# Eighteen subtractions moved from GpSimd to VectorE, and eight scalar products from GpSimd to ScalarE, in an attention and mixture-of-experts kernel

## The chip, the cores and the metric

One of the eight cores of one Trainium2 chip runs the whole program. The metric is device time in microseconds (us). Before the change the kernel takes 1013.66 us, the median of three runs (1013.41 to 1014.27). Engines are named as in the profile: PE is TensorE's matmul, PEld its weight load, DVE is VectorE, ACT is ScalarE, POOL is GpSimd, SP is the engine that issues most DMAs.

## The reference

Two parts follow each other. The first is attention inside clusters, for 4 batches of 8 heads, 768 tokens and 64 numbers a head:

```
q_assign = argmax(normalized q . normalized centroids);  k_assign likewise
scores = q . k^T / sqrt(64), -1e9 where the two clusters differ
attn   = softmax(scores);   attn_out = attn . v
```

The second takes the 3072 tokens with all their heads side by side (512 numbers) as x:

```
logits = x @ w_gate + log1p(exp(x @ w_noise)) * noise
the two best of 8 experts per token, softmax weights over these two
out[token] += weight * (relu(x @ w1[e]) @ w2[e])
```

## The kernel before, in words

Numbers of 32 bits are carried as two halves of 16 bits (upper and lower), and each product is three matmuls of halves, so nearly every tile has a step that makes its upper half and one that subtracts to get the lower.

The attention works through 16 pairs of heads, numbered 0 to 15 (`p`); four pairs are a batch `b`. A pair has 12 steps: two heads (`s`) by six blocks of 128 keys (`kc`); step number `i = 6*s + kc`. I write 7/2 for step 2 of pair 7. A step does this:

- `scores` (L641, L642): PE multiplies one key block with all 768 queries (four matmuls of 384 columns), ACT takes the exponential into a 32-bit tile `pe` of 128 by 768.
- `split_p` (L653): the upper 16 bits of `pe` are used in place as the upper half; one TENSOR_TENSOR subtracts them from `pe` and writes the lower half `pl`. It has two inputs in SBUF. It stands on POOL, except for the last nine steps of pair 14 and all of pair 15, where it stands on DVE. It is issued one step after its `scores` (two or three steps late in a few steps near the end).
- `values` (L670, L672, L676), four to five steps later: PE multiplies both halves with the halves of v and adds up in the tile `av`; 18 small matmuls, the last six with `pl`. After a head's last block DVE normalizes: `rs` (L682, from `av` and the factor `ch`), its reciprocal (L683), and the product into `xt` (L685). There is one `av` tile, so the next head's first L670 waits for L685.

Beside these steps run the preparations for the next pair: transposes of q and k (L511) with their halves on ACT (L524) and DVE (L525), the search for the cluster (L543 to L566 on the PSUM tile `aux`, ending in `oh`, which L575 transposes into the mask), and the row maxima (`b_max`: L611 on PE, L613 on DVE, two of each a step). Once per batch come the sizes of v, its halves (L467, L468 on ACT, L469 on POOL), and `x_scale`, whose last part `heads` writes the two numbers `ch` of a partition: `am` times `xsc` (L455). Pair 0 uses `am` itself; from pair 1 on L682 needs `ch`. The two writes stand once per batch, in pairs 1, 4, 8 and 12.

The second half's routing is spread under the attention: each pair's output is split (L720, L721) and stored, transposed back (L1189) and multiplied with the gate (L739); `g_gate` is a chain of small DVE steps on `aux`; and when a batch's places are known, twelve list writes (`g_list`, L898 and L899: a MEMSET of one number and an indirect DMA, both on POOL) put its tokens into the table `tbl`. For batch 0 these fall into pairs 7 to 9, for batch 1 into pairs 11 to 13, for batch 2 into pairs 14 and 15. After some 460 us the experts start; from there on PE is busy without a pause.

The order on each engine is written by hand: `at(step, f)` puts each piece into a third of a step by the numbers of the table `AT`, and every engine executes its own instructions in that order. The main loop is

```
slot(0)
scores(t)
split_p(t - 1)
slot(1)
values of step t - 4
slot(2)
```

The PSUM buffers `ring` (six of them) go round among `scores`, `b_max`, the transposes and the small products, so a reader that is late holds up a PE matmul some six buffers later.

Of the kernel before, what the change touches and what calls it, by code (L numbers as in the profile page):

```python
# [14 lines left out]
AF = mybir.ActivationFunctionType  # L15
OP = mybir.AluOpType
# [19 lines left out]
    vd=[1, 1, 2, 3, 4, 5], sec=-6.0, qf=[0, -4.0], place1=4.333,  # L36
    fv=[{'v': -5.0, 'vscale': 13.0, 'am': 24.333, 'amstep': 0.333, 'vsplit': 25.333, 'vstep': 2.0},
        {'v': 9.0, 'vscale': 11.667, 'am': 13.333, 'amstep': 0.333, 'xs': 14.0, 'vsplit': 15.0, 'vstep': 1.0}],
    wmax=42, thr=0.333, bmax1=14.667, bstep1=0.5)


def rap(tensor, offset, dims):
# [3 lines left out]
class Kernel:  # L46
# [402 lines left out]
    def x_scale(self, b):  # L449
        nc = self.nc  # L450

        def heads():
            self.ch[b] = self.wk.tile([128, 2], F32, name="ch")
            for g in range(2):
                nc.gpsimd.tensor_scalar(self.ch[b][:, g:g + 1], self.am[b, g][:, 1:2], self.xsc[:, b, 0:1], None,  # L455
                                        op0=OP.mult)

        return self.power_root(self.wk, lambda: self.vm[b], lambda: self.xsc[:, b], 2) + [heads]

# [185 lines left out]
    def split_p(self, p, s, kc):  # L645

        nc, st = self.nc, self.st[p]
        pe = st["p", s, kc].rearrange("p a n -> p (a n)")
        hi = pe.bitcast(BF).rearrange("p (n two) -> p n two", two=2)[:, :, 1]
        lo = self.wk.tile([128, self.S], F16, name="pl", bufs=5)  # L650

        last = p == self.NP - 1 or (p == self.NP - 2 and 6 * s + kc >= 3)
        (nc.vector if last else nc.gpsimd).tensor_tensor(lo, pe, hi, op=OP.subtract)  # L653
        st["p", s, kc] = hi, lo

    def values(self, p, s, kc):
# [674 lines left out]
```

## Time and profile before

| what | us |
|---|---|
| median of three runs | 1013.66 |
| the profiled execution's own time | 1013.59 |
| its span, first to last instruction | 1011.8 |
| PE busy in the span | 928.7 (92%) |
| DVE busy | 660.6 (65%) |
| POOL busy | 565.7 (56%) |
| ACT busy | 473.4 (47%) |

The span of the profile is 1.79 us shorter than that execution's own time, and this execution is within 0.1 us of the median. The shares are means over two parts with different limits: up to some 460 us all four engines are loaded, behind it PE alone. The busy time of PE is modelled at the matmuls' ends, so a PE that is busy throughout may still follow another engine's pace. A number in brackets at the end of a timeline row is the idle time of the engine before it, with what ended it.

### The profile page before, as it was taken

Reading aid. Unit: us, or ns where it says so; the run is one execution under the profiler, and the core shown is the slowest. Engines: PE = TensorE matmul, PEld = TensorE weight load, DVE = VectorE, ACT = ScalarE, POOL = GpSimd, SP = SyncE. Lnnn points to the kernel's source line nnn. Section 1 sums busy time; section 2 is a strip of 40 time slices with the busy share of each in tenths; the row PEclk is TensorE's granted clock in tenths of the full one; section 3 lists DMA queues with packets and bytes.
Section 4 is the critical chain, followed back from the end, with each engine's and each line's share of the span. In section 5 each row is a group of like instructions: output and inputs, shape, how many; then the busy total and the mean of one; then the engine's idle time right before and its main releaser. Section 6 shows DMA issues by size and latency. Waiting matters only on the chain.

```text
span 1011.8 us, 22606 instructions
## 1 busy us (share of the span) xinstructions
PE 928.7 (92%) x8825; PEld 560.4 (55%) x8825; DVE 660.6 (65%) x1485; ACT 473.4 (47%) x896; POOL 565.7 (56%) x608
## 2 busy tenths in 40 slices
PE   4588989898899987889999999999999999999997
PEld 3356666666666664668555445455454454554543
DVE  6688777888678876897556465365564654655631
ACT  4578788888787865674032224123131241231310
POOL 9268797979997899853456125242261252422312
PEclk7699999999999998999999999999999999999999
DMA  6543767666667444668377645655665356555201
GB/s 178 125 118 89 194 156 185 183 165 145 179 153 189 119 95 98 204 152 176 109 150 242 137 142 167 140 174 149 173 193 140 126 165 152 172 151 155 73 24 46
DMA packets 181905, 148.84 MB, mean 147 GB/s; under 512 B 93543, under 2 KB 159079, under 8 KB 181794
## 3 DMA queue, kind: packets, MB, share of 16 engines
q1 hardware_dynamic: 167990, 110.73, 43.8%
q0 software_dynamic: 13296, 36.38, 11.7%
q8 instruction: 70, 1.15, 0.5%
q10 hardware_dynamic: 508, 0.25, 0.1%
q14 instruction: 41, 0.34, 0.1%
HBM read 81.80 MB, written 26.12 MB: 107 GB/s over the span
## 4 chain that ended last, share of the span: by engine, by line
PE 57%; POOL 10%; DVE 9%; issue 9%; ACT 6%; DMA 4%; SPq 0%; ACTq 0%; POOLq 0%; DVEq 0%
PE ring L1230 21%; PE ring L1270 20%; POOL pl L653 6%; PE ring L641 5%; ACT pe L642 3%; DVE mm L613 3%; PE ring L611 2%; POOL tbl L899 2%; DMA B<-nt 2%; PE av L670 1%; PE av L676 1%; PE av L672 1%; POOL out L1283 1%; PE ring L1260 1%; DVE pl L653 1%
## 5 line engine op out<-in xcount | busy, mean ns | idle before, releaser
L653 POOL TENSOR_TENSOR pl<-pe 128x768 f16<-128x768 f32 x171 | 247.9, 1468 | 47.4 <-ACT pe L642 41.9
L1230 PE MATMUL ring<-xT,w1t 128*128 128x404 f16 (+2 forms) x1632 | 267.1, 324 | 0.0
L1270 PE MATMUL ring<-w2t,hT 128*128 128x512 f16 x1152 | 250.8, 379 | 0.5 <-DVE w2t L1166 0.5
L642 ACT ACTIVATE pe<-ring,sc 128x384 f32<-128x384 f32 x384 | 200.0, 577 | 69.1 <-PE ring L641 62.0
L613 DVE TENSOR_REDUCE mm<-ring 128x1 f32<-128x384 f32 x384 | 192.1, 549 | 44.6 <-PE ring L611 44.0
L1283 POOL DMA_INDIRECT out<-yo,idx x52 | 58.7, 1129 | 285.4 <-DVE yo L1279 209.3
L1230 PEld LDWEIGHTS <-w1t 128*128 128x128 f16 x1632 | 157.4, 97 | 106.4 <-issue 2.5
L1270 PEld LDWEIGHTS <-hT 128*128 128x128 f16 x1152 | 112.4, 98 | 135.0 <-issue 1.2
L1239 ACT ACTIVATE hT<-ring 128x404 f16<-128x404 f32 (+2 forms) x136 | 57.6, 469 | 202.1 <-PE ring L1230 201.9
L641 PE MATMUL ring<-B 128*128 128x384 f16 x384 | 127.2, 332 | 3.6 <-DMA B<-nt 3.6
L641 PE MATMUL ring<-A 128*128 128x384 f16 x384 | 126.8, 330 | 3.6 <-ACT pe L642 2.1
L611 PE MATMUL ring<-A 128*128 128x384 f16 x384 | 105.2, 334 | 16.5 <-ACT pe L642 8.0
L1240 DVE SCALAR_TENSOR_TENSOR hT<-ring,hT 128x404 f16<-128x404 f32 (+2 forms) x136 | 66.7, 529 | 73.5 <-ACT hT L1239 73.5
L1279 DVE SCALAR_TENSOR_TENSOR yo<-ring,lsw,xt 128x512 f32<-128x512 f32 (+1 forms) x49 | 36.7, 748 | 110.2 <-PE ring L1270 104.3
L670 PE MATMUL av<-vv,pe 128*128 128x65 f16 x1152 | 96.9, 194 | 7.5 <-DVE xt L685 7.4
L672 PE MATMUL av<-vv,pe 128*128 128x64 f16 x1152 | 96.9, 193 | 0.0
L670 PEld LDWEIGHTS <-pe 128*128 128x128 bf16 x1152 | 83.7, 98 | 22.9 <-issue 9.3
L1165 ACT ACTIVATE w1t<-stg,ws 128x1024 f16<-128x1024 f32 x32 | 34.5, 1139 | 121.2 <-DVE ws L170 121.2
L672 PEld LDWEIGHTS <-pe 128*128 128x128 bf16 x1152 | 78.4, 99 | 11.3 <-issue 4.7
L676 PE MATMUL av<-vv,pl 128*128 128x65 f16 x1152 | 66.8, 194 | 5.6 <-POOL pl L653 4.2
L1210 POOL DMA_INDIRECT xh<-xs,idx x52 | 56.4, 1085 | 16.5 <-issue 15.0
L1154 DVE TENSOR_REDUCE wm<-stg 128x1 f32<-128x1024 f32 x56 | 65.5, 1208 | 0.0
(227 smaller groups left out, 1171.0 us busy)
## 6 DMA issues: line engine op xcount, KB each, us to landing
stg<-in_moe_w SPq DMA_DIRECT2D x64, 512.0 KB
vt<-in_v SPq DMA_DIRECT2D x8, 768.0 KB
out<-zt SPq DMA_DIRECT2D x12, 512.0 KB
A<-hl SPq DMA_DIRECT2D x30, 192.0 KB
B<-hl SPq DMA_DIRECT2D x30, 192.0 KB
xs<-xh SPq DMA_DIRECT2D x15, 384.0 KB
qk<-in_q SPq DMA_DIRECT2D x7, 768.0 KB
qk<-in_k SPq DMA_DIRECT2D x7, 768.0 KB
```

Of the source, the lines that this page charges most:

```text
L611: nc.tensor.matmul(t, A[:, 0, s, j * 128:j * 128 + 128], A[:, 1, s, n * 384:n * 384 + 384], start=True, stop=True)
L613: nc.vector.tensor_reduce(st["mm"][:, c, n:n + 1], t, axis=X, op=OP.max, negate=True)
L641: nc.tensor.matmul(t, M[:, 1 - qi, s, ks], M[:, qi, s, ns], start=not qi, stop=bool(qi))
L642: nc.scalar.activation(pe[:, n], t, AF.Exp, bias=math.log(64.0), scale=st["sc"][:, 4:5])
L653: (nc.vector if last else nc.gpsimd).tensor_tensor(lo, pe, hi, op=OP.subtract)
L670: nc.tensor.matmul(av[:, j, :], ph[:, js], vv[:, hh, kj, 64:129], start=(kc == 0 and j == 0), stop=False, skip_group_check=True)
L672: nc.tensor.matmul(av[:, j, :64], ph[:, js], vv[:, hh, kj, 0:64], start=False, stop=False, skip_group_check=True)
L676: nc.tensor.matmul(av[:, j, :], pl[:, js], vv[:, hh, kj, 64:129], start=False, stop=(kc == NJ - 1), skip_group_check=True)
L1230: nc.tensor.matmul(p, self.w1t[:, wi, c, f * 128:f * 128 + 128], self.xT[:, c, xi, n0:n1], start=(i == 0), stop=(i == 3 * ND - 1))
L1240: nc.vector.scalar_tensor_tensor(h1, x, 0.0, h0, op0=OP.max, op1=OP.subtract)
L1270: nc.tensor.matmul(p, self.hT[:, hi, f, t * 128:t * 128 + 128], self.w2t[:, wi, f], start=(i == 0), stop=(i == 3 * NF - 1))
L1283: i = nc.gpsimd.indirect_dma_start(out=self.out, out_offset=bass.IndirectOffsetOnAxis(ap=en[:r], axis=0), in_=yo[:r], in_offset=None, boun ...
```

## The change

In six pairs (7, 8, 9, 11, 12, 13) the steps 2, 6 and 10 take their lower half on DVE instead of POOL: 18 of the 171 that stand on POOL. And `heads` writes `ch` by two ACTIVATEs on ACT instead of two TENSOR_SCALARs on POOL, once per batch.

```
-    wmax=42, thr=0.333, bmax1=14.667, bstep1=0.5)
+    wmax=42, thr=0.333, lists=(7, 8, 9, 11, 12, 13), bmax1=14.667, bstep1=0.5)
...
             for g in range(2):
-                nc.gpsimd.tensor_scalar(self.ch[b][:, g:g + 1], self.am[b, g][:, 1:2], self.xsc[:, b, 0:1], None,
-                                        op0=OP.mult)
+                nc.scalar.activation(self.ch[b][:, g:g + 1], self.am[b, g][:, 1:2], AF.Copy, scale=self.xsc[:, b, 0:1])
...
-        last = p == self.NP - 1 or (p == self.NP - 2 and 6 * s + kc >= 3)
-        (nc.vector if last else nc.gpsimd).tensor_tensor(lo, pe, hi, op=OP.subtract)
+        i = 6 * s + kc
+        vector = (p == self.NP - 1 or (p == self.NP - 2 and i >= 3) or
+                  (p in AT["lists"] and i % 4 == 2))
+        (nc.vector if vector else nc.gpsimd).tensor_tensor(lo, pe, hi, op=OP.subtract)
```

The changed file has one line fewer between L455 and L650 and one more behind that: what was L613 is L612 there, L653 is L654, L682 is L683, L898 is L899. PE and SP keep their order.

On DVE, in pair 7 around step 3 (mm are the row maxima, mx the first step of the cluster search), before:

```order
L849 SCALAR_TENSOR_TENSOR rec<-aux,xsc,gm 128x6
L613 TENSOR_REDUCE mm<-ring 128x1 x6
L549 TENSOR_REDUCE mx<-aux 128x24
L495 TENSOR_REDUCE ring<-ring 128x2
L182 TENSOR_SCALAR ring<-ring 128x2
L497 TENSOR_SCALAR sc<-ring 128x2
```

The same place with the change:

```order
L850 SCALAR_TENSOR_TENSOR rec<-aux,xsc,gm 128x6
L612 TENSOR_REDUCE mm<-ring 128x1 x4
L654 TENSOR_TENSOR pl<-pe 128x768
L612 TENSOR_REDUCE mm<-ring 128x1 x2
L548 TENSOR_REDUCE mx<-aux 128x24
L494 TENSOR_REDUCE ring<-ring 128x2
```

The split of 7/2 now stands ahead of two row maxima and of the whole cluster search. Those of 7/6 and 7/10 stand likewise between row maxima, the first of them behind `oh`.

On POOL, in pair 7 where batch 0's list writes begin (vv is the lower half of v, tbl the table), before:

```order
L653 TENSOR_TENSOR pl<-pe 128x768 x2
L469 TENSOR_TENSOR vv<-vt,vv 128x12x64
L898 MEMSET spacer 1x1
L899 DMA tbl<-rec,pk 32768x2
L653 TENSOR_TENSOR pl<-pe 128x768 x2
```

With the change:

```order
L654 TENSOR_TENSOR pl<-pe 128x768 x2
L468 TENSOR_TENSOR vv<-vt,vv 128x12x64
L899 MEMSET spacer 1x1
L900 DMA tbl<-rec,pk 32768x2
L654 TENSOR_TENSOR pl<-pe 128x768
```

Between two list writes stand now one split and two splits in turn, where there were always two.

On ACT, in pairs 4, 8 and 12 (hl are the halves of q and k of the next pair), with the change:

```order
L641 ACTIVATE pe<-ring,sc 128x384 x2
L523 ACTIVATE hl<-ring,sc 128x384
L455 ACTIVATE ch<-am,xsc 128x1 x2
L523 ACTIVATE hl<-ring,sc 128x384
L641 ACTIVATE pe<-ring,sc 128x384 x2
```

Before, the two of hl followed each other and `ch` stood on POOL between two splits.

## Rows read from the trace of the kernel before

**Rows 1.** The chain that ended last, 236 to 281 us, its shares by line.
```profile
by line: POOL pl L653 58.1%; POOL tbl L899 18.4%; POOL xh L721 7.1%; issue 5.8%; ACT pe L642 3.6%; PE ring L641 1.5%; DVE xt L685 1.3%; PE av L670 1.2%; PE av L672 0.8%; PE av L676 0.8%; POOL ch L455 0.6%; DVE rs L682 0.5%; POOL spacer L898
```

**Rows 2.** Pairs 7, 8 and 12: stretch, length, busy PE, PEld, DVE, ACT, POOL, then clock.
```profile
225.90:252.10 26.20, 23.26 (x368) 16.76 (x365) 22.34 (x60) 22.11 (x42) 22.53 (x23) 1.00 0.62 148
252.10:280.70 28.60, 23.25 (x371) 17.04 (x368) 19.47 (x51) 22.08 (x42) 27.25 (x31) 1.00 0.76 180
...
358.70:387.80 29.10, 24.98 (x389) 17.80 (x386) 19.92 (x53) 16.81 (x35) 27.76 (x31) 0.94 0.52 104
```

**Rows 3.** Who waited for whom: us in total, times, the longest.
```profile
DVE rs L682 <- POOL ch L455: 7.6, 2, 3.8
...
PE av L676 <- POOL pl L653: 4.2, 6, 0.9
...
PE aux L543 <- DVE gm L798: 2.2, 1, 2.2
...
PE ring L739 <- DMA xhT<-xh: 1.6, 1, 1.6
```

**Rows 4.** The end of pair 8 in order of time: POOL, DVE, PE.
```profile
278.15 0.30 POOL L455 TENSOR_SCALAR ch<-am,xsc 128x1 f32<-128x1 f32 x1
...
278.49 0.23 DVE L682 TENSOR_SCALAR rs<-av,ch 128x6 f32<-128x6 f32 x1 [3.81 <-POOL ch L455]
...
279.58 0.19 PE L670 MATMUL av<-vv,pe 128*128 128x65 f16 x1 [3.05 <-DVE xt L685]
```

**Rows 5.** Stretches of 4 us; the last three numbers are PE's granted clock, DMA share, GB/s.
```profile
279.00:283.00 4.00, 3.42 (x53) 2.50 (x53) 3.05 (x7) 3.57 (x6) 3.81 (x5) 0.73 0.78 158
...
383.00:387.00 4.00, 3.49 (x37) 1.95 (x38) 1.84 (x6) 0.58 (x3) 3.82 (x7) 0.57 0.54 142
```

**Rows 6.** The tile pl: duration in ns, least, median, most.
```profile
L653 POOL TENSOR_TENSOR pl<-pe x171: 1457/1468/1486, 46.1 to 425.8; 128x768 f16<-128x768 f32 x171
L653 DVE TENSOR_TENSOR pl<-pe x21: 942/951/2335, 423.5 to 458.7; 128x768 f16<-128x768 f32 x21
```

**Rows 7.** Two DVE splits that met a POOL split, in order of time.
```profile
422.65 1.48 POOL L653 TENSOR_TENSOR pl<-pe 128x768 f16<-128x768 f32 x1
...
423.48 1.47 DVE L653 TENSOR_TENSOR pl<-pe 128x768 f16<-128x768 f32 x1
...
425.81 2.33 DVE L653 TENSOR_TENSOR pl<-pe 128x768 f16<-128x768 f32 x1
...
425.83 1.49 POOL L653 TENSOR_TENSOR pl<-pe 128x768 f16<-128x768 f32 x1
```

**Rows 8.** Pair 7, steps 2 to 4, in order of time: ACT, POOL, DVE, PE.
```profile
232.45 1.03 ACT L642 ACTIVATE pe<-ring,sc 128x384 f32<-128x384 f32 x2
...
233.42 1.59 POOL L469 TENSOR_TENSOR vv<-vt,vv 128x768 f16<-128x768 f32 x1
...
232.08 1.02 DVE L613 TENSOR_REDUCE mm<-ring 128x1 f32<-128x384 f32 x2 [0.91 <-PE ring L611]
234.06 1.02 DVE L613 TENSOR_REDUCE mm<-ring 128x1 f32<-128x384 f32 x2 [0.95 <-PE ring L611]
...
240.74 0.45 PE L575 MATMUL ring<-identb,oh 128*128 128x128 bf16 x5 [0.74 <-DVE oh L566]
```

**Rows 9.** Pair 7, step 7, and the start of pair 8: DVE and PE.
```profile
243.78 0.62 DVE L525 SCALAR_TENSOR_TENSOR hl<-ring,sc,hl 128x384 f16<-128x384 f32 x1
...
244.82 0.49 PE L511 MATMUL ring<-ident,qk 128*128 128x128 f32 x3
...
254.04 0.56 DVE L613 TENSOR_REDUCE mm<-ring 128x1 f32<-128x384 f32 x1 [2.42 <-PE ring L611]
```

**Rows 10.** The small ACTIVATE nearest in form to the new ch.
```profile
L845 ACT ACTIVATE rec<-aux,xsc 128x6 f32<-128x6 f32 x4 | 1.1, 272 | 4.8 <-DVE pk L844 4.8
```

**Rows 11.** POOL held by a DVE operation with two inputs in SBUF: POOL, DVE.
```profile
486.26 1.45 POOL L877 TENSOR_TENSOR ent<-lg,tokn 128x168 f32<-128x168 f32 x1
...
485.89 1.48 DVE L1166 SCALAR_TENSOR_TENSOR w2t<-stg,ws,w2t 128x1024 f16<-128x1024 f32 x1
```

## The prediction

> **What bounds the kernel now.** I read the chain of waits first, then the busy time pair by pair, then the waits, then the order of time at the places they name. Behind 460 us PE works without a pause on the experts, so whatever the attention wins or loses goes through to the end at its full size.
>
> The chain from 236 to 281 us is POOL: 58.1% of it are splits, 18.4% list writes, and PE stands there only at the last [rows 1]. The same picture comes back for batch 1. By pairs: pair 7 takes 26.20 us, pair 8 28.60, pair 12 29.10, and in the two long ones POOL is busy 27.25 and 27.76 us, practically all the time, while DVE is busy only 19.47 and 19.92 [rows 2]. So POOL, with twelve splits and some six list writes a pair, falls behind.
>
> What this lateness costs shows in the waits [rows 3]: DVE stood 7.6 us in two waits for `ch`, PE 4.2 us in six waits for `pl`, and 1.6 us for one transposed xhT, whose lower half POOL makes late. The first `ch` is a 0.3 us operation that starts at 278.15, behind the late splits; DVE idles 3.81 us before L682, and PE 3.05 us for L685 [rows 4]. Right after that PE's clock is granted at 0.73 over four us, and at 0.57 after the same place in pair 12: part of the time at 1.2 instead of 2.4 GHz, each time after PE had stood [rows 5].
>
> The other engine to watch is DVE. In pair 7 it is busy 22.34 of 26.20 us [rows 2], and 1.86 of the 3.86 us left lie in two pieces ahead of step 4 [rows 8]. PE follows closely: L575 waits 0.74 us for the cluster search [rows 8], and in step 7 a transpose starts at 244.82 on a buffer that DVE's L525 left at 244.40 [rows 9], 0.42 us of room. DVE's idle time lies at a pair's start: 0.91 and 0.95 us before the row maxima of pair 7 [rows 8], 2.42 us at the start of pair 8 [rows 9].
>
> **The change part by part.**
>
> *ch on ACT.* Eight TENSOR_SCALARs leave POOL, eight ACTIVATEs come to ACT. The nearest row is an ACTIVATE of six numbers a partition with a scale from a tile, 272 ns [rows 10], so two cost at most 0.54 us and, being of one number, perhaps 0.4. They stand between the two halves of hl; L525 on DVE comes 0.4 later, which the 0.42 us of room in the same position of a pair [rows 9] covers. Without that cover it would be 0.4 us in each of three pairs. Their inputs `am` and `xsc` come from DVE pieces that stand steps earlier in the order. With them DVE's 7.6 us go, and PE's 3.05. In pair 12 PE's stop stands under xhT, 1.6 us, and goes too, since POOL is no longer late there. What is late next in pair 13 is the gate's chain: PE's 2.2 us for `gm` [rows 3]. I leave that as it is.
>
> *The clock.* After the two stops the clock lost 4 x 0.27 = 1.1 us and 4 x 0.43 = 1.7 us of PE's work [rows 5]. DVE and ACT kept their pace meanwhile, so I count 1.7 of these 2.8 us as gain; ends 0 and 2.8.
>
> *Splits off POOL.* 18 x 1.468 = 26.4 us leave POOL [rows 6], three in each pair. POOL is busy 27 us in its worst pair, so some 23 are left of 25 to 26. The six waits for `pl` go: 4.2 us. The end on the other side: DVE can hold POOL as well. L877 ran 1.45 us from 486.26 and ended 0.34 us behind DVE's L1166, which had run from 485.89 [rows 11]. With 0.95 us of such a hold per split POOL gains 0.5 us each instead of 1.47, 9 us in all over six pairs, and about half of the 4.2 would stay.
>
> Gain together: 3.05 + 1.6 + 1.7 + 4.2 = 10.5 us; ends 6 and 13 (the latter with 2.8 of clock and most of the `gm` wait).
>
> *Splits on DVE.* 18 x 0.951 = 17.1 us come to DVE [rows 6]. Each has its place among the row maxima, and what stands behind it waits: the reduces, then `ring` buffers, then PE.
>
> Step 10 (six splits): they end up in the idle time of the next pair's start, 2.42 us in pair 8 [rows 9]. Counted at nothing; without that cover 0.95 each.
>
> Step 2 (six): the split can start when the reduces of 232.08 are done (233.10) and the exponential of 7/2 is (233.48), and the next reduce was at 234.06 [rows 8]. Alone it would end at 234.5, 0.4 us late. But POOL's L469 holds 233.42 to 235.01 [rows 8], and two DVE splits that met a POOL split took 1.47 and 2.33 us: they ended 0.82 us after POOL's (422.65 + 1.48 = 424.13 against 424.95; 427.32 against 428.14) [rows 7]. So this one ends at 235.8, 1.8 us behind 234.06. From there DVE works without idle to `oh`, and L575 waited for `oh` already, so all 1.8 reach PE. Pair 11 has the same order on POOL and DVE, L469 included, and I take the same: 3.6 us for both. In pairs 8, 9 and 12 no L469 stands there, and idle time like the 0.95 us of pair 7 covers the split: 0.1 us.
>
> The Trainium skill, page "SBUF — State Buffer", section "SBUF: two separate sides", says that GpSimd and a VectorE operation with two SBUF inputs take a shared port pair for a whole instruction each, and that "the other fully blocks". Rows 7 and 11 agree in both directions. Taken over all 18 splits, that rule makes the first rival below.
>
> Step 6 (six): no idle time in front. 0.951 less the 0.42 us of room [rows 9] is 0.5 us in pairs 7, 8, 11 and 12; in pair 9, which carries a gate's chain on DVE beside it, I count no room, 0.9. Sum 2.9.
>
> Pair 13's steps 2 and 6 stand inside the gate's chain, which PE waits for: 1.3 us for both, after what idle DVE has there.
>
> Meetings with a POOL split elsewhere: once POOL has caught up, its split follows each exponential at once, and where DVE takes the step POOL has nothing to do. I take 0.3 us for all.
>
> Cost together: 3.6 + 0.1 + 2.9 + 1.3 + 0.3 = 8.2 us; ends 3 (no meeting at all, some of step 6 covered) and, if each of the twelve splits of steps 2 and 6 met a POOL split at its middle, 12 x (0.95 + 0.7) = 20 less some 4 of cover, 16.
>
> **Sum.** 8.2 - 10.5 = -2.3 us, against the profiled execution's own 1013.59 (0.1 under the median): 1011.3 us, as two large numbers that nearly cancel.
>
> **The rivals.**
>
> *The meetings decide: slower.* Every split of steps 2 and 6 finds POOL in a split, because list writes keep POOL late and its splits back to back. Place: the row maxima of steps 3 and 7. Price: ten splits beside the two already counted, 0.7 us each (half a POOL split), 7 us in place of 0.3. Time 1011.3 + 6.7 = 1018. It decides from a mean meeting of 0.5 us upward (then 5 in place of 0.3, and the result is over 1015.6 with the clock falling once more). For it: POOL is busy 22 to 27 us of a pair [rows 2], and both rows where it could be seen show it [rows 7]. Against: three splits fewer a pair leave gaps exactly where DVE's splits stand. Chance 0.24.
>
> *DVE has more room than I give it.* The steps 2 and 6 cost what they cost without POOL, and PE's own pace hides half of it: cost 3 instead of 8.2, time 1006. For it: DVE's stops before L682 go, which hands it 7.6 us in pairs 8 and 12. Against: pairs 7, 9 and 11 have no such stop. Chance 0.20.
>
> *One bound for another.* POOL, held by DVE, keeps half of its waits (2.1 us) and pairs 7, 9 and 11 lose what 8 and 12 win: 1011.3 + 2.1 = 1013.4, no change. Chance 0.16. That the change doesn't do what it says I exclude: the order on each engine shows all 18 and all eight moved.
>
> **How the numbers follow.** A measurement of this kernel tells about 0.2%, 2 us, from no change: 1011.6 to 1015.7 is "same". My forecast has 0.40; its own range is 1008.5 to 1014. Of it 0.23 lie below 1011.6 and 0.17 in "same". The second rival is faster (0.20), the third same (0.14) or a little to either side (0.01 each), the first slower (0.23) or at the edge (0.01). Faster 0.44, same 0.32, slower 0.24. The range reaches from the second rival at 1006 to near the first at 1017.5.
>
> **What would show it.** Right: no DVE wait for `ch`, no PE wait for `pl` from POOL in pairs 7 to 12, pairs 8 and 12 two to three us shorter, pairs 7 and 11 one to two us longer with L575's wait near 2.5 us, clock 1.0 around 280 and 385 us. DVE's splits: median near 0.95 us, those of 7/2 and 11/2 near 2.2. Wrong: a mean of the 18 above 1.4 us (then the first rival), or pairs 7 and 11 no longer than before (then the second); new waits of POOL's splits on DVE would speak for the third. A granted clock that falls in pairs 7 or 11 would be a cost that I have left out.

## The result, and the profile after

The changed kernel takes 1021.52 us (median of four runs, 1021.26 to 1021.99) against 1013.96 (median of four, 1013.41 to 1014.61): a ratio of 1.0075, 95% interval 1.0057 to 1.0092. It is 7.6 us slower; the forecast was 1011.3 and its range ended at 1017.5, so the time lies outside it. The profiled execution's own time is 1021.99 us, its span 1020.1.

I measured each pair of heads in both traces, from its first scores to those of the next pair (us):

| pair | 7 | 8 | 9 | 10 | 11 | 12 | 13 |
|---|---|---|---|---|---|---|---|
| before | 26.24 | 28.57 | 26.13 | 25.87 | 26.04 | 29.05 | 27.69 |
| after | 26.81 | 27.66 | **34.09** | 26.72 | 26.84 | 27.81 | 28.58 |

Pair 9 alone loses 7.96 us, about as much as the whole result; the others together lose 1.0. The page's line of busy time has, against the table of before, 28 us more on DVE and 28 less on POOL:

```profile
PE 929.2 (91%) x8825; PEld 558.6 (55%) x8825; DVE 688.9 (68%) x1503; ACT 475.0 (47%) x904; POOL 537.5 (53%) x582
```

POOL's work fell by what 18 splits and eight small products take, 26.4 and some 2 us. DVE's grew by more than the 17.1 us that 18 splits take alone, and by pairs (7, 8, 9 and 12; columns as in [rows 2]) one sees where:

```profile
226.75:253.56 26.81, 23.47 (x370) 16.52 (x366) 24.38 (x61) 21.45 (x41) 22.95 (x23) 1.00 0.58 146
253.56:281.22 27.66, 23.97 (x370) 16.74 (x367) 26.32 (x57) 20.28 (x39) 23.55 (x25) 1.00 0.66 172
281.22:315.31 34.09, 25.69 (x369) 17.51 (x366) 28.82 (x62) 24.21 (x48) 19.66 (x15) 0.90 0.59 136
...
368.87:396.68 27.81, 24.18 (x388) 17.14 (x385) 25.82 (x59) 18.40 (x38) 22.71 (x24) 1.00 0.49 108
```

DVE is busy 26.32 of 27.66 us in pair 8, where it had 19.47 of 28.60, and POOL is down from 27.25 to 23.55. The view of the tile `pl` shows what is new (duration in ns: least, median, most; first and last start):

```profile
L654 POOL TENSOR_TENSOR pl<-pe x153: 1455/1467/2102, 46.1 to 433.8; 128x768 f16<-128x768 f32 x153
L654 DVE TENSOR_TENSOR pl<-pe x39: 942/950/6735, 234.5 to 467.1; 128x768 f16<-128x768 f32 x39
```

DVE's median is still 0.95 us, as in [rows 6], but one split took 6.735 us. Taken over 226 to 425.2 us, where the 18 moved ones stand, the view of groups (busy us, mean ns; idle time before them and its end) has

```profile
L654 DVE TENSOR_TENSOR pl<-pe 128x768 f16<-128x768 f32 x18 | 32.4, 1802 | 2.6 <-ACT pe L641 2.6
```

so they took 32.4 us in all, not the 17.1 that 18 x 0.951 makes. By step: 2.24, 2.70, 6.74, 2.23, 2.71 and 1.35 us in step 2 of pairs 7, 8, 9, 11, 12 and 13; 0.95 to 0.97 in every step 6; 2.66, 0.95, 1.47, 1.79, 0.95 and 0.95 in step 10. The extra 15.3 us are 12.3 in step 2 and 3.1 in step 10.

The longest, 9/2, in order of time (start, duration, engine): DVE, then POOL, then PE.

```profile
289.92 6.74 DVE L654 TENSOR_TENSOR pl<-pe 128x768 f16<-128x768 f32 x1 [1.60 <-ACT pe L641]
296.58 1.01 DVE L612 TENSOR_REDUCE mm<-ring 128x1 f32<-128x384 f32 x2
```
```profile
286.12 0.98 POOL L900 DMA_INDIRECT tbl<-rec,pk  x1 [0.16 <-issue]
287.13 2.89 POOL L654 TENSOR_TENSOR pl<-pe 128x768 f16<-128x768 f32 x2
289.99 1.58 POOL L468 TENSOR_TENSOR vv<-vt,vv 128x768 f16<-128x768 f32 x1
291.53 4.30 POOL L654 TENSOR_TENSOR pl<-pe 128x768 f16<-128x768 f32 x3
```
```profile
297.18 0.94 PE L610 MATMUL ring<-A 128*128 128x384 f16 x2 [5.80 <-DVE mm L612]
```

DVE's split starts while POOL is in the second split of the row at 287.13 (a row here is a run of POOL operations without a pause). That one ends at 290.02, and DVE does not come in: `vv` and three more splits follow on POOL without a pause, to 295.83, and DVE ends at 296.66, 0.83 us behind the last. Row maxima stand behind it on DVE, and PE stands 5.80 us for them. The clock then falls (stretches of 4 us; the number behind POOL's is the granted clock):

```profile
279.00:283.00 4.00, 3.71 (x56) 2.48 (x56) 3.62 (x8) 3.97 (x8) 0.01 (x1) 1.00 1.00 171
294.00:298.00 4.00, 0.82 (x3) 0.30 (x3) 4.00 (x5) 0.00 (x0) 1.84 (x2) 0.53 0.50 169
298.00:302.00 4.00, 3.91 (x46) 2.38 (x45) 3.83 (x14) 2.38 (x5) 1.00 (x1) 0.62 0.01 4
383.00:387.00 4.00, 3.52 (x55) 2.45 (x54) 3.90 (x11) 3.03 (x6) 3.62 (x7) 1.00 0.04 7
```

PE works again from 297.18 on, at 1.2 GHz for part of the stretch that was granted 0.62 (0.38 x 4 = 1.5 us of its work lost). The stretches of [rows 5] are at 1.00 now: what the clock lost there was won back, and lost again in pair 9. From pair 7's first scores to pair 14's the granted clock averages 0.97 in both traces.

POOL's row of splits is nothing that the change made. The kernel before has it at the same time, only there nobody waited for it:

```profile
287.06 2.89 POOL L653 TENSOR_TENSOR pl<-pe 128x768 f16<-128x768 f32 x2
289.91 1.58 POOL L469 TENSOR_TENSOR vv<-vt,vv 128x768 f16<-128x768 f32 x1
291.45 5.73 POOL L653 TENSOR_TENSOR pl<-pe 128x768 f16<-128x768 f32 x4
```

The moved splits had let POOL catch up, and that was lost at once. In the trace after, POOL stood until 284.34 for ACT's upper half of v:

```profile
284.34 1.59 POOL L468 TENSOR_TENSOR vv<-vt,vv 128x768 f16<-128x768 f32 x1 [5.32 <-ACT vv L467]
```

In the kernel before the same operation started at 284.25, without a wait:

```profile
284.25 1.60 POOL L469 TENSOR_TENSOR vv<-vt,vv 128x768 f16<-128x768 f32 x1
```

From there on POOL is equally late in both.

### The profile page after: what moved, and what is told of

Read it like the earlier page. It is cut to its first block, busy times and chain, and to the rows that moved or that the text cites. A ratio compares the mean times of both kernels' runs of the same rounds, so it can differ in the third digit from the quotient of the medians.

```text
span 1020.1 us, 22610 instructions
## 1 busy us (share of the span) xinstructions
PE 929.2 (91%) x8825; PEld 558.6 (55%) x8825; DVE 688.9 (68%) x1503; ACT 475.0 (47%) x904; POOL 537.5 (53%) x582
## 4 chain that ended last, share of the span: by engine, by line
PE 58%; DVE 14%; issue 9%; ACT 7%; DMA 4%; POOL 2%; SPq 0%; ACTq 0%; POOLq 0%; DVEq 0%
PE ring L1231 21%; PE ring L1271 20%; PE ring L640 5%; ACT pe L641 4%; DVE mm L612 4%; DVE pl L654 3%; PE ring L610 3%; DMA qk<-in_q 2%; PE av L671 2%; PE av L677 1%; PE av L673 1%; PE ring L510 1%; DMA B<-nt 1%; POOL out L1284 1%; PE ring L1261 1%
## 5 line engine op out<-in xcount | busy, mean ns | idle before, releaser
L654 POOL TENSOR_TENSOR pl<-pe 128x768 f16<-128x768 f32 x153 | 223.6, 1475 | 62.8 <-ACT pe L641 54.7
L612 DVE TENSOR_REDUCE mm<-ring 128x1 f32<-128x384 f32 x384 | 191.9, 547 | 31.9 <-PE ring L610 31.4
L610 PEld LDWEIGHTS <-A 128*128 128x128 f16 x384 | 36.9, 99 | 50.3 <-issue 27.3
```

What stands on the lines that cost most here:

```text
L610: nc.tensor.matmul(t, A[:, 0, s, j * 128:j * 128 + 128], A[:, 1, s, n * 384:n * 384 + 384], start=True, stop=True)
L612: nc.vector.tensor_reduce(st["mm"][:, c, n:n + 1], t, axis=X, op=OP.max, negate=True)
L654: (nc.vector if vector else nc.gpsimd).tensor_tensor(lo, pe, hi, op=OP.subtract)
```

## The experiments

The ratio of each kernel is to the kernel before on the same chip, with its 95% interval. The ten kernels stand on three chips, so ratios are compared between them, not medians. A trace is that of one execution; where pair 7 starts differs between the traces by up to 3 us (225.87 to 228.96) though no split is moved ahead of it, so lengths of pairs are compared, not where they stand.

### One half of the change each

`ch` on ACT alone, no split moved:

```
-                  (p in AT["lists"] and i % 4 == 2))
+                  False)
```

> Only the two ACTIVATEs for ch; all 18 splits stay on POOL. Theory (the forecast's gains were right, the port was not): DVE's 7.6 us of waits for ch go, PE's 3.05 and 1.6 with them, while the six waits for pl stay; 1008 to 1011 against 1014.0. Rival (POOL paces these pairs anyway, so that the wait for ch is replaced by waits for pl): within 1.5 us of the kernel before.

Measured: 1012.58 us against 1014.45, ratio 0.9979 (0.9968 to 0.9989): 1.9 us, between what the theory and what the rival named. The 18 splits alone, with `ch` back on POOL:

```
-                nc.scalar.activation(self.ch[b][:, g:g + 1], self.am[b, g][:, 1:2], AF.Copy, scale=self.xsc[:, b, 0:1])
+                nc.gpsimd.tensor_scalar(self.ch[b][:, g:g + 1], self.am[b, g][:, 1:2], self.xsc[:, b, 0:1], None, op0=OP.mult)
```

> Only the 18 splits on DVE; ch stays on POOL. Theory: the splits cost what the whole change costs, and ch is not late any more once POOL has fewer splits, so the time is within 1 us of the changed kernel's 1021.5. Rival (ch on ACT is worth 3 us here too): 1024 or more.

Measured: 1022.69 us, ratio 1.0088 (1.0074 to 1.0102); pair 9 takes 34.08 us. So the splits make the loss, and `ch` on ACT wins 2 us where 3 to 6 were expected. With the splits alone DVE has no wait for `ch` either, though POOL writes it. The trace of `ch` alone shows how PE's 3.05 us of [rows 4] were lost again: pair 8 is 2.3 us shorter, and pair 9 takes 29.65 us, 3.5 more, with another wait at almost the same time. (This execution, 1014.17 us, was slower than nine of the other ten, so the trace may show more of it than the median has.) Its PE, then SP:

```profile
282.31 0.48 PE L640 MATMUL ring<-B 128*128 128x384 f16 x1 [2.37 <-DMA B<-nt]
```
```profile
276.69 0.72 SPq L581 DMA_DIRECT2D B<-nt  x1
277.52 4.04 SPq L1190 DMA_TRANSPOSE xhT<-xh  x1
```

The transfer of `nt` into B, which pair 9's scores need, is issued at 276.69, and PE stands for it until 282.31; the matmul then lasts 0.48 us, where one at full clock lasts 0.32 or 0.33. The clock's gain is not had either: over pair 9 the granted clock is 0.88, where it was 0.93 before. A transpose is issued right behind it; that this slows the transfer I did not test.

### Is it 9/2 alone?

The change with 9/2 back on POOL:

```
-                  (p in AT["lists"] and i % 4 == 2))
+                  (p in AT["lists"] and i % 4 == 2 and (p, i) != (9, 2)))
```

> The change, with the split of 9/2 alone back on POOL (17 moved). Theory: one DVE split that stands in the port's queue for 6.7 us makes nearly all of the loss, so the time falls by 6 to 8 us, to 1013.5 to 1015.5. Rival (DVE is full in all six pairs, and the long stop only shows it): it falls by less than 3 us.

Measured: 1021.39 us, ratio 1.0065 (1.0051 to 1.0079). The theory's 6 to 8 us are missed. The rival's number came, but not by its reason: the stop did not go, it moved to the next moved split, 9/6, which had taken 0.95 us in the change. DVE, then POOL:

```profile
300.64 5.53 DVE L654 TENSOR_TENSOR pl<-pe 128x768 f16<-128x768 f32 x1
```
```profile
299.44 1.64 POOL L722 TENSOR_TENSOR xh<-xt,xh 128x768 f16<-128x768 f32 x1
301.05 4.30 POOL L654 TENSOR_TENSOR pl<-pe 128x768 f16<-128x768 f32 x3
```

DVE waits through `xh` and three splits and ends 0.82 us behind them; PE stands 4.58 us. In the change 9/6 was short: POOL had worked off its row behind PE's long stop and stood idle 1.78 us, up to the split that followed at 305.85.

Pair 9 left out altogether:

```
-    wmax=42, thr=0.333, lists=(7, 8, 9, 11, 12, 13), bmax1=14.667, bstep1=0.5)
+    wmax=42, thr=0.333, lists=(7, 8, 11, 12, 13), bmax1=14.667, bstep1=0.5)
```

> The change without pair 9: 15 splits moved. Theory after the first runs (POOL has caught up, then stands for the first half of v in pair 8, and the splits that pile up behind it keep the port from whichever DVE split of pair 9 comes next): without pair 9 nothing waits there, 1014 to 1016. Rival (the loss is spread over all six pairs): 1019 or more.

Measured: 1014.80 us, ratio 0.9999 (0.9987 to 1.0012), pair 9 25.98 us. Against the change's 1.0075 the loss of 7.6 us is gone: it stands in pair 9, and taking out one of its splits was not enough. The other 15 splits win nothing, though: `ch` alone is at 0.9979.

### Which step of a pair?

The condition `i % 4 == 2` was replaced by `i == 2`, by `i == 6` and by `i == 10`; `ch` stays on ACT.

> Of the 18 splits only the six of step 2, ch on ACT. Theory (steps 2 and 6 of a pair cost, step 2 most, since DVE meets POOL's half of v there): 1016 to 1020, with the long stop in 9/2. Rival (no place is dear by itself, POOL's backlog decides): under 1014.

> Only the six of step 6, ch on ACT. Theory: they mostly ran in 0.95 us in the changed kernel, and cost 0.5 us each: 1012 to 1016, unless 9/6 now meets the backlog. Rival (no place is dear by itself): as the kernel with ch alone, 1011 to 1013.

> Only the six of step 10, ch on ACT. Theory (they fall into the idle time of DVE at the next pair's start): no dearer than ch alone, 1010 to 1013. Rival (DVE's delay reaches PE here as well): 1014 to 1017.

| steps on DVE | us | ratio (interval) | the six splits, us | pair 9, us |
|---|---|---|---|---|
| 2 | 1019.29 | 1.0047 (1.0032 to 1.0062) | 9/2 6.72, the others 2.0 to 3.1 | 33.46 |
| 6 | 1017.57 | 1.0034 (1.0021 to 1.0047) | 9/6 5.52, 7/6 3.42, 11/6 3.20, 8/6 2.34, two 0.95 | 32.63 |
| 10 | 1010.73 | 0.9962 (0.9947 to 0.9977) | 7/10 3.47, 8/10 2.61, 9/10 1.39, 11/10 3.26, 12/10 1.23, 13/10 0.95 | 26.47 |

Steps 2 and 10 came as their theories had it; step 6 lies above its 1012 to 1016, and 9/6 did meet the late POOL, as was left open there. Against `ch` alone (0.9979) step 2 costs 0.0068, 6.9 us, step 6 costs 0.0055, 5.6 us, and step 10 wins 1.7 us, though the intervals of step 10 and of `ch` alone overlap. With step 10 alone the kernel is faster than both others. Its splits are held too, 12.9 us for six instead of 5.7 (18.3 with step 2, 16.4 with step 6). Two things keep it cheap: its split in pair 9 meets one POOL split alone (1.39 us), and what stands behind a held split is less urgent to PE. Splits held as long show the second: behind 7/6 (3.42 us) and 11/6 (3.20) PE waits 1.74 and 1.53 us for row maxima, behind 7/10 (3.47) not at all and behind 11/10 (3.26) 0.83 us, the only such wait with step 10 alone. PE behind 7/6, then behind 11/10:

```profile
247.27 0.79 PE L610 MATMUL ring<-A 128*128 128x384 f16 x2 [1.74 <-DVE mm L612]
```
```profile
362.16 0.32 PE L640 MATMUL ring<-A 128*128 128x384 f16 x1 [0.83 <-DVE mm L612]
```

The first one of step 10, in pair 7, DVE, then POOL:

```profile
253.03 3.47 DVE L654 TENSOR_TENSOR pl<-pe 128x768 f16<-128x768 f32 x1
256.42 1.94 DVE L612 TENSOR_REDUCE mm<-ring 128x1 f32<-128x384 f32 x4
```
```profile
252.77 2.90 POOL L654 TENSOR_TENSOR pl<-pe 128x768 f16<-128x768 f32 x2
255.60 0.09 POOL L899 MEMSET spacer<- 1x1 f32 x1
255.87 1.49 POOL L900 DMA_INDIRECT tbl<-rec,pk  x1 [0.18 <-issue]
```

DVE meets one POOL split and is passed by the next, which started about 1.2 us after DVE's. Behind them comes a list write, POOL idles 0.18 us before its DMA, and DVE is in: it ends at 256.50, 0.83 us behind the second. Pairs 8 and 12 of this kernel, to be read against [rows 2]:

```profile
254.50:280.41 25.91, 23.60 (x370) 16.88 (x367) 22.87 (x54) 19.24 (x38) 24.71 (x26) 1.00 0.72 187
359.64:386.72 27.08, 23.56 (x388) 17.33 (x385) 23.10 (x56) 17.35 (x37) 25.73 (x28) 1.00 0.52 105
```

They are 2.7 and 2.0 us shorter, which is the gain that the forecast hoped for there.

### What lets DVE in?

If any other operation between two of POOL's splits ended the hold, a small one would do. The change with a MEMSET of one number behind each POOL split of pair 9:

```
+        if p == 9 and not vector:
+            nc.gpsimd.memset(self.spacer, 0.0)
```

> The change, and in pair 9 a MEMSET of one number on POOL behind each split that stands on POOL. Theory: DVE gets the port as soon as an operation without an SBUF input stands between two of POOL's, so the split of 9/2 takes 0.9 to 2.5 us instead of 6.7 and the time falls by 5 to 8 us. Rival (DVE waits until POOL has nothing left to do): 9/2 still takes over 6 us, time within 1 us of 1021.5.

Measured: 1022.54 us, ratio 1.0086 (1.0072 to 1.0100). DVE, then POOL:

```profile
289.12 6.81 DVE L654 TENSOR_TENSOR pl<-pe 128x768 f16<-128x768 f32 x1 [1.60 <-ACT pe L641]
```
```profile
290.74 1.46 POOL L654 TENSOR_TENSOR pl<-pe 128x768 f16<-128x768 f32 x1
292.15 0.09 POOL L656 MEMSET spacer<- 1x1 f32 x1
292.20 1.46 POOL L654 TENSOR_TENSOR pl<-pe 128x768 f16<-128x768 f32 x1
293.60 0.09 POOL L656 MEMSET spacer<- 1x1 f32 x1
```

Three MEMSETs stand between the operations that pass, and DVE still waits: a miss for that version. No idle time shows before any of them. The next kernel makes POOL really stop: behind each moved split it copies one number of the lower half that DVE writes, so it waits until DVE's split is done.

```
+        if vector and p in AT["lists"]:
+            nc.gpsimd.tensor_copy(self.spacer, lo[0:1, 0:1])
```

> The change with one POOL operation added behind each of the 18 moved splits: a copy of one number of the lower half that DVE writes, so that POOL's queue stops there until DVE's split is done. Theory (a DVE split that waits for the SBUF port is passed over by POOL operations that follow each other without a pause, and comes in as soon as POOL's queue stops): in pair 9, step 2, DVE waits only for POOL's 9/0, vv and 9/1, so the split takes about 3.9 us instead of 6.7 and PE's stop of 5.8 us shrinks to about 3; every other of the 18 lasts at most one POOL operation longer, 2.5 us; the 18 together take 26 to 28 us instead of 32.4. Time 1018 to 1019.5 us against 1021.5. Rival (the hold is not ended by a stop of POOL's queue but by the backlog being worked off): 9/2 stays above 6 us and the time at 1021.5. A third outcome is possible: POOL, now tied to DVE, is late itself and the time stays though 9/2 is short.

Measured: 1018.58 us (1018.12 to 1022.61, six runs), ratio 1.0053 (1.0035 to 1.0070). Its interval overlaps the change's, and two of the six runs (1021.91 and 1022.61) are no faster than it, so the time alone doesn't settle it. The trace shows what became of the hold. DVE, POOL, PE:

```profile
288.92 3.90 DVE L654 TENSOR_TENSOR pl<-pe 128x768 f16<-128x768 f32 x1 [1.60 <-ACT pe L641]
```
```profile
288.99 1.58 POOL L468 TENSOR_TENSOR vv<-vt,vv 128x768 f16<-128x768 f32 x1
290.53 1.46 POOL L654 TENSOR_TENSOR pl<-pe 128x768 f16<-128x768 f32 x1
292.95 0.18 POOL L656 CAST spacer<-pl 1x1 f32<-1x1 f16 x1 [0.96 <-DVE pl L654]
```
```profile
293.33 0.79 PE L610 MATMUL ring<-A 128*128 128x384 f16 x2 [2.96 <-DVE mm L612]
```

9/2 takes 3.90 us, PE stops 2.96, pair 9 takes 31.28 us, and the 18 splits 28.1: close to what the theory named, though 7/10 and 11/10 took 2.91 and 2.90, above its 2.5. DVE comes in where POOL's queue stops, and `vv` and 9/1, which stand ahead of the stop, still pass it.

That POOL waits for DVE's own result is not needed; idle time is enough. The trace of the change has 9/10 coming in behind one POOL split, before 0.55 us of idle time with no list write near. POOL, then DVE:

```profile
315.06 1.47 POOL L654 TENSOR_TENSOR pl<-pe 128x768 f16<-128x768 f32 x1 [2.04 <-ACT pe L641]
317.08 1.59 POOL L654 TENSOR_TENSOR pl<-pe 128x768 f16<-128x768 f32 x1 [0.55 <-ACT pe L641]
```
```profile
315.87 1.47 DVE L654 TENSOR_TENSOR pl<-pe 128x768 f16<-128x768 f32 x1
```

A list write's DMA that is under way is not always enough. 8/2 started in one and was still passed by the split behind it:

```profile
259.90 0.98 POOL L900 DMA_INDIRECT tbl<-rec,pk  x1 [0.17 <-issue]
260.92 1.48 POOL L654 TENSOR_TENSOR pl<-pe 128x768 f16<-128x768 f32 x1
```
```profile
260.51 2.70 DVE L654 TENSOR_TENSOR pl<-pe 128x768 f16<-128x768 f32 x1
```

7/10 and 12/2 did so as well (2.66 and 2.71 us); 8/6 and 12/6, which started some 0.35 us into such a DMA and not 0.6, took 0.95. What makes the difference is open.

### A version with two splits at a pair's end

Steps 10 and 11 in pairs 7, 8, 11 and 12:

```
-                  (p in AT["lists"] and i % 4 == 2))
+                  (p in AT["lists"] and i >= 10))
```

with `lists=(7, 8, 11, 12)`.

> ch on ACT, and steps 10 and 11 instead of 2, 6 and 10 on DVE, in pairs 7, 8, 11 and 12 alone (8 splits in place of 18). Theory (a held DVE split costs nothing where DVE's next operations have slack, as at the end of a pair, and costs its whole wait where PE stands behind the row maxima): both splits are hidden in DVE's idle time at the next pair's start, pairs 8 and 12 lose POOL's lateness, and the time is 1010 to 1012 us, 0.996 to 0.998 of the kernel before, like the run with step 10 alone. Rival (the room at a pair's start holds one split and not two): the row maxima of the next pair's start come 2 to 3 us late in each of four pairs, and the time is 1016 us or more.

Measured: 1014.67 us (1013.46 to 1016.13), ratio 0.9997 (0.9988 to 1.0006). Neither fits. From pair 7's first scores to pair 14's this trace takes 187.8 us, the one with step 10 alone 186.3 and the kernel before 189.6, so the two splits are not quite hidden; that both reach pair 14 at 414.5 to 414.6 us comes from pair 7, which starts 1.5 us earlier here. Pair 12 alone takes 29.94 us instead of 27.08. Both of its held splits make PE wait for row maxima:

```profile
360.18 0.32 PE L640 MATMUL ring<-A 128*128 128x384 f16 x1 [0.83 <-DVE mm L612]
363.37 0.32 PE L640 MATMUL ring<-A 128*128 128x384 f16 x1 [0.49 <-DVE mm L612]
```

PE's wait for `xhT` there is 2.4 us instead of 1.7. The rest of the difference lies in the experts' part: the last `values` end at some 458.3 us in both traces, and the span of this one ends 2.1 us later, where PE's waits sum up to 1.7 us more. The trace of the kernel in which POOL waits for DVE, from the same chip, is nearly as late in that part (1.9 us), so this need not come from the splits; no trace shows whether the kernel before does the same on that chip, and I leave the cause open. It is no better than step 10 alone.

## Why the prediction was wrong

**The step that failed** is the cost of a meeting. [Rows 7] and [rows 11] were read as a wait for one POOL operation, the one that DVE meets. With that, the prediction put 1.8 us each on 7/2 and 11/2, 0.1 on the other splits of step 2 and "0.3 us for all" on other meetings. The runs show a wait to the end of POOL's row, with DVE done 0.8 us behind it. In 7/2 and 11/2 the row ended with the operation that was met, `vv` before a list write, and they took 2.24 and 2.23 us, as worked out. In 9/2 four operations followed the one that was met; it took 5.8 us above 0.95, and PE's wait of 5.80 us behind it is most of the 7.96 that pair 9 lost. 8/2 and 12/2, counted as covered, took 2.70 and 2.71, as a split passed them too. The Trainium skill's sentence on the shared port pair (page "SBUF — State Buffer", section "SBUF: two separate sides"), that "the other fully blocks", agrees with each trace on the blocking. It has the one that starts first hold the pair for its own instruction; here the wait went on through four more, and the runs decide.

**A row misread.** "In pairs 8, 9 and 12 no L469 stands there": in pair 9 it did, at 289.91, in the middle of 10 us of POOL without a gap. I took the place of POOL's operations from pair 7, where POOL was early, and not from pair 9, where it ran some two steps late. A look at POOL's idle time around 290 us would have shown it.

**The cost was counted in the wrong step.** Step 6 was forecast at 2.9 us for 0.951 less some room, and in the change all six take 0.95 to 0.97 us: no TENSOR_TENSOR of POOL was under way when they started. Moved alone, step 6 costs 5.6 us, held up to 5.52. What a split costs depends on where POOL stands at that moment, and this on the stops before it: taking out 9/2 only handed its wait to 9/6. Step 10 "at nothing" came nearly true, and in part by luck: six splits of 0.95 us were counted, and they are held for up to 3.47 us alone and 2.66 in the change, where PE waits 1.1 us behind three of them.

**The gains** of 10.5 us were too high. No DVE wait for `ch` and no PE wait for `pl` from POOL is left, as forecast, but pairs 8 and 12 win 0.9 and 1.2 us instead of two to three. In place of those waits stand others for DVE. From pair 7's first scores to pair 14's the change has, among others:

```profile
PE av L671 <- DVE xt L686: 1.4, 3, 0.5
PE ring L610 <- DVE sc L498: 1.1, 2, 0.5
PE ring L610 <- DVE gl L746: 1.1, 2, 0.5
```

The change without pair 9 has the same three (1.5, 1.1 and 1.1 us), which may be why its 15 splits win nothing. `ch` alone wins 1.9 us (1014.45 against 1012.58), and its trace shows the stop at 280 us followed by another one, for a DMA. The `xhT` wait at the end of pair 12 stays, 1.3 us against 1.6 [rows 3], and so does `gm`'s, 2.2 us. `ch` on ACT costs what was said: eight ACTIVATEs of 291 ns, and neither DVE nor PE waits for them.

**The rivals.** "The meetings decide" had the mechanism, its place and its sign, at 1018 and a chance of 0.24. Its mark, a mean of the 18 above 1.4 us, came true with 1.80. It was short by 3.5 us, because it priced each meeting at half a POOL split and knew no wait through several. Pairs 7 and 11 grew by 0.6 and 0.8 us, less than the one to two us named: of the 1.8 us put on each, 0.51 and 0.50 reach PE as a wait for row maxima, and L574 waits 0.73 us in pair 7 as L575 did before, not 2.5. That POOL would be held by DVE happened too: the longest of its splits took 2.10 us instead of 1.47, but PE waited for none in pairs 7 to 13.

## What to carry to other kernels

An operation that another engine's operations can hold (here a TENSOR_TENSOR on DVE with two inputs in SBUF, beside POOL) is to be priced by that engine's longest stretch without idle time around its place, not by its own duration nor by one operation of the other. Read the stretch at every place, since the same step of the next pair can meet another one. Put such operations where nothing urgent stands behind them on their engine: here a split of the same form cost nothing behind 3.47 us of waiting at a pair's end, and 5.80 us of PE in the middle of one. And when a late engine is relieved, follow it to its next wait for an input: POOL won time up to 278 us and had lost it all by 284.

## What the chip showed that I had not expected

- A DVE operation that waits for POOL is passed over by POOL operations that start after it: four in a row, 6.74 us in all, where alone it takes 0.95.
- A MEMSET of 0.09 us between them does not let DVE in (6.81 us). Idle time on POOL does: 0.55 us before its next split (9/10 of the change, 1.47 us), and a stop of POOL's queue for DVE's own result (9/2, 3.90 us). The places with 0.16 to 0.18 us of idle time before a list write's DMA let it in too; whether idle time as short as that is enough without the DMA was not tried.
- In four of the twelve traces (the kernel before, `ch` alone, the splits alone, the change without pair 9) the granted clock over pair 15 is 0.93, and PE takes 23.4 to 23.7 us from its first scores to its last `values`; in the other eight it is 1.00 and 22.1 us. Part of the difference between two traces, up to 1.6 us, is this and not the splits of pairs 7 to 13; why the clock falls there in some is open.
